# A spectral layer and an MLP on one core: the first forward stage ahead of the weight loads, and later forward stages moved beside their own middle stage

## The chip, the cores and the metric

The kernel runs on one core of one Trainium2 chip. The metric is the device time of one execution in microseconds (us), as the median of several runs of the same program. Everything below is read from one execution that the hardware profiler recorded. PE is the matmul engine (PEld its weight loads), DVE the vector engine, ACT the scalar engine, POOL the GpSimd engine, SP the engine that issues most of the DMAs.

## The reference, cut to what matters

```python
X = np.fft.rfft(x, axis=1)                    # x: 8 batches x 3008 x 256, f32
Yr = Xr @ w_r - Xi @ w_i + b_r                # 256 x 256 complex product per frequency
Yi = Xr @ w_i + Xi @ w_r + b_i
Yr = np.sign(Yr) * np.maximum(np.abs(Yr) - 0.01, 0.0)   # the same for Yi
y = np.fft.irfft(Yr + 1j * Yi, n=3008, axis=1)
h = y.reshape(24064, 256) @ w_in              # 256 x 2048, float64 data
out = np.maximum(0.01 * h, h) @ w_out         # 2048 x 256, float64 data
```

## The kernel before, in words

The transform of 3008 = 47 x 64 points is done as two small transforms. For each batch b there are three pieces of work ahead of the MLP.

- `fwd(b)`, the first stage: x is read as seven column steps c of 2 x 256 columns in two halves h (the last is half as wide). `fold` adds and subtracts the halves, `stage_a` multiplies by the 120 x 120 matrix `fa`, ACT copies the result out of PSUM, and a DMA writes it to the buffer `u_dram` in device memory.
- `mid(b)`, the middle stage: 12 steps j. Each reads a tile `u` back from `u_dram` in another order (`load`), does the second transform (`stage_b`, with `fb`), the complex product with `w_r`, `w_i` (`proj`: `kc`, `t`, `c`, `zf`), the threshold on DVE, the first inverse transform (`stage_g`, with `gb`) and writes `v` to `v_dram`.
- `inverse` and `forms`: read `vin` from `v_dram`, finish the inverse transform, and split 512 tokens into the operands `yh`, `yl` of the MLP.

The MLP (`moe_a`, `moe_b`, `moe_o`) runs over 47 chunks of 512 tokens in eight steps q each. `w_in` and `w_out` arrive as float64 bits and are turned into pairs of f32 by `convert_win` (four quarters, on ACT and DVE) and `load_wout` (eight pieces).

Batches 0 and 1 are prepared ahead (`NPRE` = 2): batch 0 by `f0` and `m0` before the MLP, `fwd(1)` by `fp` in the shadow of `m0`. From then on `Stream` objects hand out the work of later stages in proportion to the progress of the MLP. In the main loop `cur` counts batches; while the MLP passes from one batch to the next, the streams are `fwd(cur + 2)` and then `mid(cur + 1)`. So `fwd(b)` is written one interval ahead of `mid(b)`. The first interval (`cur` = 0) is the shortest: it spans four chunks, its first fifth is left out, and the others span almost six.

Engines run their instructions in the order of the built program, and each DMA queue (SP's and ACT's) issues in order; an instruction that waits holds everything behind it on its engine. The final order is made by a scheduler from the order of the code, so it is shown below from the built programs.

In the part before the MLP the places of interest are: line 648, the first quarter of `w_in` loaded right behind x; lines 664 to 673, the second quarter and the first conversion; lines 676 to 685, the other quarters; line 689, conversions three and four inside `m0`; line 702, `split_consts`, which splits six constants into pairs for the later stages.

Of the kernel before, what the change touches and what calls it, by code (L numbers as in the profile page):

```python
# [8 lines left out]
F32 = mybir.dt.float32  # L9
# [9 lines left out]
N1, N2, NK1 = 47, 64, 24  # L19
# [11 lines left out]
def spectral_mlp_kernel(  # L31
# [173 lines left out]
    XT = [("gf", 2)] + [("gl", 2)] * 2 + [("gh", 2)] * 2 + [("yc", 2)] * 2  # L205
    XT1 = [("yc", 2)] * 2 + [("gf", 2), ("gh", 2), ("yl", 2), ("yh", 2), ("gh", 2)]

    def fwd(b):
# [3 lines left out]
        x_t, s_t = {}, {}  # L212

        def load(c):
            cols = slice(2 * c * D, min(2 * c + 2, NS) * D)
            n = cols.stop - cols.start
            if b < NPRE:
                tag, bufs = (XT, XT1)[b][c]
                x2 = sb.tile([PA, 2, 2 * D], F32, name="xin", tag=tag, bufs=bufs)
                x_t[c] = [x2[:, h, :n] for h in range(2)]  # L220
            else:
                x_t[c] = [
                    sb.tile([PA, 2 * D], F32, name=f"xin{h}", tag="uv"[h], bufs=3 - h)[:, :n] for h in range(2)
                ]
            for h, t in enumerate(x_t[c]):
                if b == 0:
                    (act if h else sync).dma_start(t, x[b, h, :, cols])
                else:
                    with tc.issue_after(reads[-1].ins):
                        sync.dma_start(t, x[b, h, :, cols])  # L230
# [19 lines left out]
        def stage_a(c, h):  # L250
            t = x_t[c][h]
            n = t.shape[1]
            pa = (bank("psf", 2) if b else bank("psh", 4))[:PA, :n]
            products(pa, [(consts[f"fa{h}"] if b else consts[f"fa{h}32"], s_t[c][h])])
            t = x_t[c][1 - h]
            cp = act.copy(t, pa)
            if b == 0:
                turned[:] = [cp]
            st = (act if b else sync).dma_start(uv[h, :, 2 * c * D:2 * c * D + n], t)
            if b == 0:  # L260
                written.append(st)
# [22 lines left out]
        ahead = 2 if b >= NPRE else NX  # L284
        for c in range(ahead):
            load(c)
# [17 lines left out]
    def mid(b):  # L304
# [111 lines left out]
        yield 0  # L416
# [71 lines left out]
    def forms(ci):  # L488
# [7 lines left out]
        def split(k, w):  # L496
            act.copy(yh[:, k], w)  # L497
            return dve.tensor_sub(yl[:, k], w, yh[:, k].bitcast(F32))  # L498
# [12 lines left out]
        if ci == 0:  # L511
            made[:] = [last]
# [135 lines left out]
    load_win(0, (sync, act))  # L648
    load_plain("fb", fb, [P, NK1 + 1, N2])
    load_weights()  # L650
# [6 lines left out]
    sync.dma_start(consts["gb32"][0], gb)  # L657
# [6 lines left out]
    load_win(1, (sync, sync), written[7])  # L664
# [4 lines left out]
    act.copy(bz[:1], brow[:1])  # L669
    act.copy(bz[32:33], brow[32:33])  # L670
    dve.tensor_sub(bz[32:33], brow[32:33], bz[32:33].bitcast(F32))
    act.mul(fa32[:, 2], fa32[:, 1], -1.0)
    convert_win(0)
    m0 = Stream(mid(0), MID)
    m0.to(0.001)
    for c in range(2, 4):
        load_win(c, (sync, sync), reads[3])
# [6 lines left out]
    with tc.issue_after(turned[0].ins):  # L684
        convert_win(1)
# [16 lines left out]
    with tc.issue_after(thresholded[-1].ins):  # L702
        split_consts()
# [3 lines left out]
    next(wout)  # L707


    mids = [Stream(mid(b), MID) for b in range(1, NB)]  # L710
    cur, streams = -1, ()
    for i, pos in enumerate(moe()):
# [3 lines left out]
        if i in (2, 4):  # L716
            with tc.issue_after(made[0].ins):
                next(fp.gen)
        while cur + 1 < NB - 1 and pos >= (read[cur + 1] if cur >= 0 else 0):
# [3 lines left out]
            streams = ([Stream(fwd(cur + NPRE), FWD)] if cur + NPRE < NB else []) + [mids[cur]]  # L723
# [111 lines left out]
```

## Time and profile before

| What | us |
|---|---|
| median of 3 runs | 2609.61 |
| lowest and highest | 2607.25, 2610.03 |
| the profiled execution | 2609.83 |
| its span, first to last instruction | 2608.0 |
| PE busy within the span | 2543.3 |
| DVE, ACT, POOL busy | 1884.8, 1654.5, 248.2 |

The page gives each engine's busy time and share. The table of stretches gives for each stretch the busy time and count of instructions of each engine, the granted clock of the matmul engine as a share of 2.4 GHz, the busy share of the DMA engines and the bytes moved per second. The timeline gives start, duration, engine, line, operation, tiles and count, and in brackets the idle time just before with what ended it. A queue's own issues carry a q (SPq, ACTq).

### The profile page before, as it was taken

To read this page: it belongs to the slowest core of one execution; us is meant where nothing else is said; L and a number is where in the kernel's file an instruction comes from. 1 tells how busy PE (TensorE), PEld (TensorE's weight loads), DVE (VectorE), ACT (ScalarE), POOL (GpSimd) and SP (SyncE) were. 2 spreads that over 40 slices of the span, in tenths; PEclk is the share of its full clock that TensorE was granted. 3 is DMA by queue.
4 is the path that set the end of the run, shared out by engine and by line. 5 is a ranking of instruction groups with operands and counts; after the bars stand their busy time and mean duration, and the time that the engine had idled before them with its cause. 6 is when DMAs were issued, how large, how long until landed. Compare 5 with 4: busy or idle time off the path is not lost.

```text
span 2608.0 us, 42647 instructions
## 1 busy us (share of the span) xinstructions
PE 2543.3 (98%) x16300; PEld 2283.9 (88%) x16300; DVE 1884.8 (72%) x3403; ACT 1654.5 (63%) x3174; POOL 248.2 (10%) x180
## 2 busy tenths in 40 slices
PE   5899999999999999999999999999999999999999
PEld 3678887999989999899999999999999999989998
DVE  6697667777787777777777777777777767667665
ACT  4665665676656666567665766666666666655554
POOL 0002102100120001200021000211000000000000
PEclk8999999999999999999999999999999999999999
DMA  8634113211142112312123111231111111100000
GB/s 248 172 99 116 53 42 92 84 52 47 32 120 61 48 37 56 101 53 59 33 74 94 52 45 41 74 94 52 45 41 53 41 41 44 42 18 32 9 17 17
DMA packets 119914, 165.14 MB, mean 63 GB/s; under 512 B 13602, under 2 KB 69918, under 8 KB 119710
## 3 DMA queue, kind: packets, MB, share of 16 engines
q1 hardware_dynamic: 79120, 115.55, 14.5%
q10 hardware_dynamic: 40589, 46.87, 7.1%
q8 instruction: 128, 2.10, 0.3%
q14 instruction: 77, 0.62, 0.1%
HBM read 86.60 MB, written 75.76 MB: 62 GB/s over the span
## 4 chain that ended last, share of the span: by engine, by line
PE 90%; DVE 3%; ACT 3%; DMA 1%; issue 1%; ACTq 0%; SPq 0%; DVEq 0%
PE pso L568 38%; PE psh L84 34%; PE psf L78 11%; PE psf L472 3%; PE psf L335 3%; DVE gl L555 1%; ACT zf L392 0%; ACT gh L553 0%; ACT gf L551 0%; DMA u_dram<-xin 0%; DVE yl L498 0%; ACT zf L388 0%; DMA raw<-w_out_dram 0%; DVE gf L549 0%; ACTq L412 0%
## 5 line engine op out<-in xcount | busy, mean ns | idle before, releaser
L84 PE MATMUL psh<-yh,win_hi 128*128 128x256 f32 x2632 | 738.4, 285 | 8.1 <-ACT yh L497 4.1
L84 PE MATMUL psh<-yl,win_hi 128*128 128x256 f32 x2632 | 735.1, 281 | 0.0
L84 PE MATMUL psh<-yh,win_lo 128*128 128x256 f32 x2632 | 727.2, 280 | 0.0
L555 DVE TENSOR_TENSOR gl<-gf,gh 128x1024 fp32r<-128x1024 f32 x376 | 475.9, 1266 | 197.5 <-ACT gh L553 195.9
L568 PE MATMUL pso<-gh,wout_hi 128*128 128x512 f32 x1504 | 596.0, 396 | 1.9 <-ACT gh L553 1.8
L568 PE MATMUL pso<-gh,wout_lo 128*128 128x512 f32 x1504 | 591.3, 393 | 0.0
L568 PE MATMUL pso<-gl,wout_hi 128*128 128x512 f32 x1504 | 559.8, 396 | 2.7 <-DVE gl L555 2.4
L84 PEld LDWEIGHTS psh<-yh,win_hi 128*128 128x128 f32 x2632 | 494.3, 189 | 33.6 <-ACT yh L497 5.7
L84 PEld LDWEIGHTS psh<-yl,win_hi 128*128 128x128 f32 x2632 | 497.1, 189 | 25.8 <-issue 0.5
L84 PEld LDWEIGHTS psh<-yh,win_lo 128*128 128x128 f32 x2632 | 493.5, 189 | 4.0 <-issue 0.2
L551 ACT ACTIVATE gf<-gf 128x768 f32<-128x768 f32 x376 | 318.6, 848 | 216.3 <-DVE gf L549 211.3
L553 ACT CAST gh<-gf 128x1024 fp32r<-128x1024 f32 x376 | 395.5, 1052 | 16.5 <-ACT gf L551 10.5
L549 DVE TENSOR_TENSOR gf<-psh,u 128x512 f32<-128x512 f32 x376 | 258.9, 689 | 198.4 <-PE psh L84 196.6
L568 PEld LDWEIGHTS pso<-gl,wout_hi 128*128 128x128 f32 x1504 | 282.5, 188 | 60.7 <-DVE gl L555 7.9
L568 PEld LDWEIGHTS pso<-gh,wout_lo 128*128 128x128 f32 x1504 | 282.9, 188 | 45.1
L568 PEld LDWEIGHTS pso<-gh,wout_hi 128*128 128x128 f32 x1504 | 283.0, 188 | 41.2 <-ACT gh L553 3.0
L548 ACT ACTIVATE gf<-psh 128x256 f32<-128x256 f32 x376 | 144.4, 384 | 214.2 <-PE psh L84 193.0
L371 POOL TENSOR_TENSOR kb<-bias,kc 128x512 f32<-128x512 f32 x84 | 121.4, 1446 | 1468.3 <-ACT kc L368 1302.2
L534 ACT COPY p<-psh 128x256 f32<-128x256 f32 x376 | 139.5, 371 | 100.0 <-PE psh L84 82.2
L535 DVE TENSOR_TENSOR u<-psh,p 128x256 f32<-128x256 f32 x376 | 157.8, 420 | 60.8 <-ACT p L534 58.2
L537 DVE TENSOR_TENSOR gf<-psh,u 128x256 f32<-128x256 f32 x376 | 157.6, 420 | 22.3 <-PE psh L84 11.1
L538 DVE TENSOR_TENSOR gf<-psh,gf 128x256 f32<-128x256 f32 x376 | 158.0, 421 | 6.8
(134 smaller groups left out, 3290.9 us busy)
## 6 DMA issues: line engine op xcount, KB each, us to landing
u<-u_dram SPq DMA_DIRECT2D x192, 128.0 KB, 2.7
v_dram<-v ACTq DMA_DIRECT2D x192, 128.0 KB, 2.4
out_dram<-ob SPq DMA_DIRECT2D x94, 256.0 KB, 2.1
vin<-v_dram SPq DMA_DIRECT2D x96, 240.0 KB, 3.5
xin<-x_dram SPq DMA_DIRECT2D x90, 240.0 KB, 3.0
u_dram<-xin ACTq DMA_DIRECT2D x72, 240.0 KB, 2.4
u_dram<-xin SPq DMA_DIRECT2D x24, 240.0 KB, 4.6
raw<-w_out_dram SPq DMA_DIRECT2D x8, 512.0 KB, 4.9
```

What stands on the lines that cost most here:

```text
L78: last = nc.tensor.matmul(dst, a, b, start=(i == 0), stop=(i == len(terms) - 1))
L84: nc.tensor.matmul(dst, a, b, start=start and i == 0, stop=i == 2, skip_group_check=True)
L534: act.copy(p1, b1[:, lo])
L535: dve.tensor_add(u2, b1[:, hi], p1)
L537: dve.tensor_add(g[:, 3], b2[:, hi], u2)
L538: dve.tensor_add(g[:, 3], b2[:, lo], g[:, 3])
L548: act.activation(g[:, 0], b1[:, lo], AF.Prelu, alpha=SLOPE)
L549: dve.tensor_add(g[:, 1:3], b2.rearrange("p (k n) -> p k n", k=2), u2.unsqueeze(1).broadcast_to([P, 2, HT]))
L551: act.activation(g[:, 1:4], g[:, 1:4], AF.Prelu, alpha=SLOPE)
L553: act.copy(gh, g)
L555: dve.tensor_sub(gl, g, gh.bitcast(F32))
L568: nc.tensor.matmul(po, a[:, f, s], r[:, i], start=(f == 0 and j == 0), stop=(f == NF - 1 and j == 2),)
```

## The change

- `fwd(0)` reads x in four pieces per half (`XW`: 2, 4, 4 and 3 column blocks of 256) in place of seven, one half by ACT's queue and one by SP's; its tiles live in `wide`. The results go back in four writes per half, all on SP's queue. `stage_a` keeps the last copy in `turned` and the last write in `written`.
- No quarter of `w_in` is loaded ahead. All four are loaded from SP's queue: the first behind the read number 3 of `u` (`reads[3]`), the others at `m0` steps 1, 5 and 8. The first conversion comes after the last copy of the first stage, the second and third at steps 5 and 10 of `m0`, the fourth after the last threshold.
- `fb` is loaded in two pieces: five of 25 blocks at the start, the rest behind `reads[3]`. `load_weights` and `gb` come behind the writes of `fwd(0)`. The casts of the bias row and `fa` follow `turned`.
- `split_consts` moves from the end of `m0` into the MLP loop (i = 8), behind the operands of the first chunk.
- For b >= 2 `fwd(b)` becomes part of the same interval as `mid(b)` and stands in front of it: the streams are `fwd(cur + 1)` (none for `cur` = 0) and `mid(cur + 1)`. `mid(b)` hands back 6 x 512 units after its first two loads, a gap for the data to land.

```diff
+    XW = [(0, 2), (2, 6), (6, 10), (10, 13)]
+    XT = ["gf", "gl", "gh", "yc"]
...
+            if b == 0:
+                lo, hi = XW[c]
+                if c == 0:
+                    x2 = sb.tile([PA, 2, 2 * D], F32, name="xin", tag=XT[c])
+                    w = [x2[:, h] for h in range(2)]
+                else:
+                    w = [sb.tile([PA, 4 * D], F32, name="xin", tag=XT[c])[:, :(hi - lo) * D] for _ in range(2)]
+                for h, t in enumerate(w):
+                    (act if h else sync).dma_start(t, x[b, h, :, lo * D:hi * D])
+                for s in range(lo, hi, 2):
+                    x_t[s // 2] = [t[:, (s - lo) * D:min(s + 2 - lo, hi - lo) * D] for t in w]
+                    wide[s // 2] = (w, lo, hi, s + 2 >= hi)
+                return
...
-            st = (act if b else sync).dma_start(uv[h, :, 2 * c * D:2 * c * D + n], t)
-            if b == 0:
-                written.append(st)
+            if b:
+                act.dma_start(uv[h, :, 2 * c * D:2 * c * D + n], t)
+                return
+            turned[:] = [cp]
+            w, lo, hi, last = wide[c]
+            if last:
+                written[:] = [sync.dma_start(uv[h, :, lo * D:hi * D], w[1 - h])]
...
         for j in range(2):
             load(j)
-        yield 0
+        yield 6 * CS if b else 0
...
-    load_win(0, (sync, act))
-    load_plain("fb", fb, [P, NK1 + 1, N2])
-    load_weights()
+    consts["fb"] = const.tile([P, NK1 + 1, N2], F32, name="fb")
+    sync.dma_start(consts["fb"][:, :5], fb[:, :5])
...
-    load_win(1, (sync, sync), written[7])
+    with tc.issue_after(written[0].ins):
+        load_weights()
+        sync.dma_start(consts["gb32"][0], gb)
...
-    convert_win(0)
     m0 = Stream(mid(0), MID)
     m0.to(0.001)
-    for c in range(2, 4):
-        load_win(c, (sync, sync), reads[3])
+    with tc.issue_after(reads[3].ins):
+        sync.dma_start(consts["fb"][:, 5:], fb[:, 5:])
+    load_win(0, (sync, sync), reads[3])
+    with tc.issue_after(turned[0].ins):
+        convert_win(0)
...
-        if i in (3, 8):
-            convert_win(2 + i // 8)
+        if i in (1, 5, 8):
+            load_win(1 + i // 4, (sync, sync), reads[-1])
+        if i in (5, 10):
+            convert_win(i // 5)
...
+    with tc.issue_after(thresholded[-1].ins):
+        convert_win(3)
...
-    with tc.issue_after(thresholded[-1].ins):
-        split_consts()
...
+        if i == 8:
+            with tc.issue_after(made[0].ins), tc.issue_after(made[1].ins):
+                split_consts()
...
-            streams = ([Stream(fwd(cur + NPRE), FWD)] if cur + NPRE < NB else []) + [mids[cur]]
+            streams = ([Stream(fwd(cur + 1), FWD + 4 * CS)] if cur else []) + [mids[cur]]
```

ACT in the first stage, before: the copies of the first stage (`xin<-psh`) with the first conversion's two ACT instructions (`cvq`, `cva`) among them.

```order
L256 COPY xin<-psh 120x512 x5
L123 ACTIVATE cvq<-win_raw 128x1024
L124 ACTIVATE cva<-win_raw 128x1024
L256 COPY xin<-psh 120x512 x5
L104 CAST wr_hi<-w_105 128x512
L669 CAST bz<-brow 1x512
L670 CAST bz<-brow 1x512
L256 COPY xin<-psh 120x512
L104 CAST gb_hi<-w_105 128x128
L256 COPY xin<-psh 120x256 x2
```

ACT at the same place, after.

```order
L268 ACT_TABLE_LOAD
L268 COPY xin<-psh 120x512 x12
L268 COPY xin<-psh 120x256 x2
L684 CAST bz<-brow 1x512
L685 CAST bz<-brow 1x512
L686 ACTIVATE fa_66<-fa_66 120x120
L353 COPY ef<-psh 128x2x256 x2
L123 ACTIVATE cvq<-win_raw 128x1024
L124 ACTIVATE cva<-win_raw 128x1024
L382 COPY kc<-pso 128x256
```

The fourteen copies now stand together; the first conversion stands behind two steps of the middle stage (`ef`) and ahead of the first copy of its product (`kc`).

SP's queue from the writes of the first stage (`u_dram<-xin`) to the first reads of the middle stage (`u<-u_dram`), before.

```order
L259 DMA u_dram<-xin 120x512 x7
L147 DMA win_raw<-w_in_dram 128x1024
L259 DMA u_dram<-xin 120x512 x3
L147 DMA win_raw<-w_in_dram 128x1024
L259 DMA u_dram<-xin 120x512
L259 DMA u_dram<-xin 120x256 x2
L321 DMA u<-u_dram 64x2x256 x6
L147 DMA win_raw<-w_in_dram 128x1024 x4
```

SP's queue there, after.

```order
L275 DMA u_dram<-xin 120x1024 x4
L275 DMA u_dram<-xin 120x768 x2
L113 DMA w_162<-w_r_dram 128x2x256
L113 DMA w_i<-w_i_dram 128x2x256
L678 DMA w_162<-gb_dram 128x128
L335 DMA u<-u_dram 64x2x256 x6
L691 DMA fb<-fb_dram 128x1280
L147 DMA win_raw<-w_in_dram 128x1024 x2
```

The `w_in` loads moved from among the writes to behind the reads; `w_r`, `w_i` and `gb` moved to between the two.

DVE at the end of `mid(0)`, before: the last two thresholds (`t`, `c`), the splits of the constants (`wr_lo` to `fa_lo`) and the last operand of `stage_g` (`zf`).

```order
L380 TENSOR_TENSOR t<-psf,kc 128x512
L383 TENSOR_SCALAR c<-t 128x512
L384 TENSOR_TENSOR t<-t,c 128x512
L105 TENSOR_TENSOR wr_lo<-w_105,wr_hi 128x512
L105 TENSOR_TENSOR wd_lo<-w_105,wd_hi 128x512
L105 TENSOR_TENSOR wn_lo<-w_105,wn_hi 128x512
L105 TENSOR_TENSOR gb_lo<-w_105,gb_hi 128x128
L105 TENSOR_TENSOR fa_lo<-fa_66,fa_hi 120x120 x2
L390 TENSOR_SCALAR zf<-t,sign 64x256 x2
```

DVE there, after.

```order
L394 TENSOR_TENSOR t<-psf,kc 128x512
L397 TENSOR_SCALAR c<-t 128x512
L398 TENSOR_TENSOR t<-t,c 128x512
L125 TENSOR_SCALAR cva<-cva 128x1024
L404 TENSOR_SCALAR zf<-t,sign 64x256 x2
L126 TENSOR_SCALAR cva<-cva 128x1024
L127 SCALAR_TENSOR_TENSOR cva<-win_raw,cva 128x1024
L128 TENSOR_SCALAR win_raw<-cva 128x1024
L125 TENSOR_SCALAR cva<-cva 128x512
```

One instruction of the fourth conversion (`cva`) stands where the six splits stood; the rest of that conversion follows behind `zf`, mixed with the first piece of `w_out`.

## Rows read from the trace of the kernel before

**Rows 1.** The page, part 1: busy time, share of the span, instructions.

```profile
PE 2543.3 (98%) x16300; PEld 2283.9 (88%) x16300; DVE 1884.8 (72%) x3403; ACT 1654.5 (63%) x3174; POOL 248.2 (10%) x180
```

**Rows 2.** Table of stretches by stage; columns in its first line.

```profile
core 0: us, PE busy (x) PEld busy (x) DVE busy (x) ACT busy (x) POOL busy (x), PEclk, DMA share, GB/s
0.00:41.60 41.60, 14.57 (x28) 6.03 (x29) 23.32 (x35) 17.99 (x31) 0.52 (x5) 0.82 0.83 253
41.60:107.80 66.20, 58.04 (x286) 47.30 (x286) 51.59 (x93) 47.76 (x96) 0.30 (x1) 0.94 0.66 186
107.80:134.50 26.70, 25.62 (x85) 13.86 (x86) 13.13 (x28) 14.47 (x32) 0.00 (x0) 0.92 0.69 207
134.50:180.00 45.50, 42.49 (x258) 35.61 (x257) 42.46 (x85) 29.91 (x57) 1.33 (x1) 1.00 0.31 99
...
220.00:480.00 260.00, 240.41 (x1499) 214.10 (x1498) 184.66 (x326) 156.77 (x311) 45.11 (x33) 0.96 0.27 76
```

**Rows 3.** Timeline of ACT in the first stage: start, duration, what.

```profile
18.80 1.12 ACT L123 ACTIVATE cvq<-win_raw 128x1024 f32<-128x1024 uint32 x1 [2.73 <-DMA win_raw<-w_in_dram]
19.82 1.10 ACT L124 ACTIVATE cva<-win_raw 128x1024 f32<-128x1024 f32 x1
20.82 2.53 ACT L256 COPY xin<-psh 120x512 f32<-120x512 f32 x5
```

**Rows 4.** Timeline of SP's queue: the first reads of the middle stage.

```profile
37.88 3.95 SPq L321 DMA_DIRECT2D u<-u_dram  x6
```

**Rows 5.** Table of stretches: DMA rates in the first stage.

```profile
2.00:14.00 12.00, 6.84 (x10) 2.79 (x11) 4.77 (x7) 3.75 (x8) 0.00 (x0) 1.00 0.99 261
14.00:22.00 8.00, 5.42 (x14) 2.13 (x13) 5.30 (x10) 4.73 (x8) 0.00 (x0) 1.00 1.03 349
...
24.00:36.00 12.00, 0.30 (x2) 0.00 (x0) 8.18 (x13) 5.38 (x11) 0.00 (x0) 0.61 0.93 306
```

**Rows 6.** DMA issues of the whole run: count, KB each, median us to landing.

```profile
u<-u_dram SPq DMA_DIRECT2D x192, 128.0 KB, 2.7
...
win_raw<-w_in_dram SPq DMA_DIRECT2D x7, 512.0 KB, 6.5
...
u_dram<-xin ACTq DMA_DIRECT2D x12, 120.0 KB, 2.3
```

**Rows 7.** Table of stretches: inside the middle stage of batch 0, and the sum.

```profile
49.00:84.00 35.00, 32.19 (x167) 25.97 (x166) 30.66 (x54) 26.84 (x55) 0.00 (x0) 1.00 0.85 238
...
sum 66.60, PE 58.04 PEld 47.33 DVE 50.98 ACT 47.51 POOL 0.30; mean PE 19.35 PEld 15.78 DVE 16.99 ACT 15.84 POOL 0.10
```

**Rows 8.** Timeline of DVE at the end of the middle stage.

```profile
103.89 0.69 DVE L384 TENSOR_TENSOR t<-t,c 128x512 f32<-128x512 f32 x1
...
106.99 0.71 DVE L390 TENSOR_SCALAR zf<-t,sign 64x256 f32<-64x256 f32 x2
```

**Rows 9.** Groups of DVE instructions, 38 to 104.6 us: the conversion's first and last.

```profile
L164 DVE TENSOR_TENSOR win_lo<-ws,win_hi 128x1024 fp32r<-128x1024 f32 x3 | 3.7, 1225 | 3.7 <-ACT win_hi L163 3.7
...
L157 DVE TENSOR_TENSOR ws<-cva 128x256 f32<-128x256 f32 x3 | 1.3, 419 | 0.0
```

**Rows 10.** PE's waits, 180 to 480 us: total, times, longest.

```profile
PE psf L78 <- DVE xz L246: 5.1, 4, 2.4
PE psh L84 <- ACT yh L497: 4.1, 2, 3.6
PE psf L78 <- DVE yt L503: 4.0, 1, 4.0
```

**Rows 11.** Chain that ended last: runs of MLP matmuls.

```profile
526.73 3.16 PE psh L84 x27
...
1263.72 2.77 PE pso L568 x12
```

**Rows 12.** Timeline at the end of fwd(2): last copy and its write.

```profile
244.80 0.37 ACT L256 COPY xin<-psf 120x256 f32<-120x256 f32 x1
...
245.21 0.32 ACTq L259 DMA_DIRECT2D u_dram<-xin  x1
```

More of the change, by code (lines that the diff above doesn't have):

```diff
@@ L204, in spectral_mlp_kernel @@
     NX = -(-NS // 2)
-    XT = [("gf", 2)] + [("gl", 2)] * 2 + [("gh", 2)] * 2 + [("yc", 2)] * 2
+    XW = [(0, 2), (2, 6), (6, 10), (10, 13)]
+    XT = ["gf", "gl", "gh", "yc"]
     XT1 = [("yc", 2)] * 2 + [("gf", 2), ("gh", 2), ("yl", 2), ("yh", 2), ("gh", 2)]
@@ L211, in fwd @@
         uv = ud.rearrange("c k (g s) d -> c (k g) (s d)", g=NG)
-        x_t, s_t = {}, {}
+        x_t, s_t, wide = {}, {}, {}
         def load(c):
@@ L216, in load @@
             n = cols.stop - cols.start
+            if b == 0:
[11 more added lines that the diff above has]
+                return
             if b < NPRE:
-                tag, bufs = (XT, XT1)[b][c]
+                tag, bufs = XT1[c]
                 x2 = sb.tile([PA, 2, 2 * D], F32, name="xin", tag=tag, bufs=bufs)
@@ L225, in load @@
             for h, t in enumerate(x_t[c]):
-                if b == 0:
[L227 to L230, printed above, removed]
+                with tc.issue_after(reads[-1].ins) if b == 1 else nullcontext():
+                    sync.dma_start(t, x[b, h, :, cols])
         def fold(c):
@@ L282, in fwd @@
             return
-        ahead = 2 if b >= NPRE else NX
-        for c in range(ahead):
+        ahead = 2 if b else NX
+        for c in range(ahead if b else len(XW)):
             load(c)
@@ L496, in split @@
         def split(k, w):
-            act.copy(yh[:, k], w)
-            return dve.tensor_sub(yl[:, k], w, yh[:, k].bitcast(F32))
+            cp = act.copy(yh[:, k], w)
+            return dve.tensor_sub(yl[:, k], w, yh[:, k].bitcast(F32)), cp
         split(0, b11)
@@ L511, in forms @@
         if ci == 0:
-            made[:] = [last]
+            made[:] = last
         yield
@@ L656, in spectral_mlp_kernel @@
     sync.dma_start(sign, sg)
-    sync.dma_start(consts["gb32"][0], gb)
     bo = sb.tile([P, 2 * D + P], F32R, name="bz", tag="t", bufs=1)
@@ L668, in spectral_mlp_kernel @@
         sb.tile([P, 4, 2, P], F32, name="ws", tag="yh"))
-    act.copy(bz[:1], brow[:1])
-    act.copy(bz[32:33], brow[32:33])
+    with tc.issue_after(turned[0].ins):
+        act.copy(bz[:1], brow[:1])
+        act.copy(bz[32:33], brow[32:33])
+        act.mul(fa32[:, 2], fa32[:, 1], -1.0)
     dve.tensor_sub(bz[32:33], brow[32:33], bz[32:33].bitcast(F32))
-    act.mul(fa32[:, 2], fa32[:, 1], -1.0)
-    convert_win(0)
     m0 = Stream(mid(0), MID)
     m0.to(0.001)
-    for c in range(2, 4):
-        load_win(c, (sync, sync), reads[3])
+    with tc.issue_after(reads[3].ins):
+        sync.dma_start(consts["fb"][:, 5:], fb[:, 5:])
+    load_win(0, (sync, sync), reads[3])
+    with tc.issue_after(turned[0].ins):
+        convert_win(0)
     bias = const.tile([P, 2, D], F32, name="bias")
@@ L683, in spectral_mlp_kernel @@
     fp = Stream(fwd(1), FWD)
-    with tc.issue_after(turned[0].ins):
-        convert_win(1)
     wout = load_wout()
@@ L706, in spectral_mlp_kernel @@
     next(wout)
-    next(wout)
-    mids = [Stream(mid(b), MID) for b in range(1, NB)]
+    mids = [Stream(mid(b), MID + 6 * CS) for b in range(1, NB)]
     cur, streams = -1, ()
```

3 lines of the change are left out of this document (removed).

## The prediction

> **What bounds the kernel now.** I read the page's busy table first. PE is busy 2543.3 us of 2608.0 [rows 1], so the end is set by PE's work, which the change leaves as it is (the built programs hold the same matmuls), and by the 64.7 us in which PE is idle, plus what it loses at half clock. So I look for where the idle time lies; the table of stretches answers [rows 2]. Up to 41.6 us PE works 14.6 us and idles 27.0. In the middle stage of batch 0 (41.6 to 107.8) it idles 8.2. While the MLP begins it idles 1.1 and 3.0, in 220 to 480 us 19.6, and 5.8 remain for all the rest. A reader should see two targets there, the start and the stretch 220 to 480, and nothing to win after 480.
>
> The start has a chain. ACT stands still 2.73 us for the first quarter of `w_in` and then converts for 2.2 us, with copies of the first stage queued behind [rows 3]. The DMA engines are busy 93 to 103% in the stretches of [rows 5], since `w_in` and `fb` share them with x and its results. Only when the last result is written does SP issue the first reads of the middle stage, at 37.88 us [rows 4].
>
> The waits of PE in 180 to 480 us [rows 10] are on DVE's and ACT's work for `fwd(2)`, `fwd(3)`, `mid(1)` and the next chunk: the first interval is the densest. The mean granted clock is 0.96 in 220 to 480 [rows 2]; two-level clock gives 260 x 0.04 x 2 = 21 us at 1.2 GHz, after such waits of 3.6 and 4.0 us. Some of it is idle anyway; I put the loss at 6 us, 26 in all with the idle time.
>
> **The change part by part.** The sum is made against the profiled 2609.83 us (span 2608.0 and 1.8 around it), 0.2 above the median of the runs.
>
> *First reads of the middle stage.* `w_in`, most of `fb` and `w_r`, `w_i` no longer stand before them. x is 13 blocks x 2 halves x 120 rows x 1 KB = 3.19 MB in, the same out, with `fa` and a fifth of `fb` 6.67 MB in all. The transfers begin near 2 us, and from the end of the last full stretch (36) to the read passed 1.9 us. At 261 GB/s (narrow x rows alone), 306 (mostly narrow writes) and 349 (with the wide rows of `w_in`) [rows 5] the bytes take 25.6, 21.8 or 19.1 us, and the read comes at 29.5, 25.7 or 23.0. I take 25.7, because half the bytes are writes as in the 306 stretch: **-12.2** (-8.4 to -14.9). The engines are not later than this: fourteen copies at 2.53/5 = 0.5 us [rows 3] follow x, which is in by 2 + 3.47/0.306 = 13.3 us, so the last write can be issued near 18, and its 0.74 MB end before 22.
>
> Rates in the trace are those of many queued transfers: 306 GB/s with pieces of 240 KB, all engines at 0.93 [rows 5]. The Trainium skill (DMA: Bandwidth & Descriptors, Bandwidth) gives for single transfers 138 GB/s at 64 KB and 341 at 1 MB and asks for 1 MiB and more. By that rule the pieces of 480 KB win more: at 341 GB/s the read would come at 2 + 19.6 + 1.9 = 23.5, an estimate from that page, and the time be 2.2 us lower. The trace does not bear it out, since its 240 KB pieces are well above what the page's table would give them.
>
> *Length of the middle stage.* Before, 66.7 us from the first read (37.88) to the end of the last threshold (104.58) [rows 4, 8]. Now the first conversion has to wait for its data behind the reads. SP issues six reads in 3.95 us [rows 4], `fb` and the two `w_in` loads at the same 0.66 each, and a `w_in` load lands 6.5 us after issue [rows 6]: some 11.8 us after the first read. Then the two ACT instructions, 2.2 us [rows 3]; DVE starts to convert at 14.0. While ACT waits, the copy `kc` of step 0 is queued behind it, on that DVE's threshold and the PSUM banks of PE's next products; but that `kc` is ready only near then, after two steps. DVE still has three conversions and twelve steps to do, as before: 51.0 us of work, the sum in [rows 7]. At the 30.66/35.00 = 88% of the busiest stretch [rows 7] that is 58.2 us, an end at 72.2: **+5.5**. If PE's pace hides it, 0 (the steps need 58 us of PE [rows 7]); at the mean share 50.98/66.60 the end is at 80.6, +13.9. I take 88%, as the conversions now fill the stage to its end.
>
> *Splits.* The six splits stand between 104.58 and 106.99 on DVE, ahead of the last `zf` [rows 8]. One instruction of the fourth conversion takes their place; a conversion's cost 0.4 to 1.2 us each [rows 9]. **-1.7** (-1.2 to -2.0). The start: -12.2 + 5.5 - 1.7 = **-8.4**.
>
> *Where the MLP begins.* The fourth conversion (twelve groups, 29.3 us for three, 9.8 each; the first and last are [rows 9]) now runs after the last threshold. DVE has 26.7 - 13.1 = 13.6 idle us there [rows 2], and PE meanwhile has `fwd(1)` to multiply, so most is covered. The splits (2.4 us) and one of the pieces of `w_out` slip into 134.5 to 180, where DVE is busy 42.46 of 45.50 and PE already waits 3.0 [rows 2]. **+2**, the splits' size (0 to +7: with a piece of `w_out`, seven DVE instructions of half the width, at 0.4 to 0.7 each [rows 9] 3 to 5 us).
>
> *First interval.* `fwd(2)` leaves it; `mid(1)` is handed out over more MLP. In the built orders, from its first `stage_b` to its last, PE has 132 us of matmuls before and 169 after, counted at 3.16/27 = 0.117 us for 256 columns and 2.77/12 = 0.231 for 512 [rows 11]; `fwd(2)` itself goes from 51 to 60. In later intervals of before a middle stage has about 190 and almost nothing is lost. So much of the 26 us should go. But the order still has tight places: at two steps only 2.4 us of matmuls between `stage_b` and the product that needs it, where before the tightest were 0.0 and 1.0; and once no matmul between the last `inverse` and the next chunk. **-10** (0 to -20, which is 26 less three waits of 2).
>
> *Six handovers.* `mid(b)` now reads what `fwd(b)` has just written. The read waits on SP's queue, ahead of output stores, `vin` and x loads. The chain: the last matmul 0.12 [rows 11], 0.41 from its copy to the issue of the write [rows 12], landing 2.3 [rows 6], a second half of the read 0.66 behind the first [rows 4], landing 2.7 [rows 6]: 6.2. The order gives 4.5, 8.1, 6.3, 6.9, 7.9 and 6.8 us of matmuls between (the first is 12 x 0.231 + 15 x 0.117), so one handover of six is short, by 1.7. **+3** with some half clock (0 to +20, if each read took the 6.5 of a `w_in` load).
>
> Sum: -8.4 + 2 - 10 + 3 = -13.4, from 2609.8 to 2596.4, or 2596 on the median.
>
> **The rivals.** *Slower: the handovers stall.* If each of the six costs 3 us of waiting and 2 of half clock, as the waits of 3.6 and 4.0 us did [rows 10], that is +30 in place of +3: 2623. For it: nothing in the kernel before reads so soon after a write except the first stage, where the read passed 1.9 us after the bytes thinned out and PE sat idle. Against: later the DMA engines are lightly used (share 0.27 in 220 to 480 [rows 2]). It decides above (8.4 - 2 + 10)/6 = 2.7 us each. Chance 0.12.
>
> *The conversions give the start back.* The same `w_in` bytes and conversions only move into the middle stage, where the DMA share is 0.85 and DVE at 88% in 49 to 84 us [rows 7]. Late reads of `u` would hold ACT and DVE in order: +13.9 for -12.2, and with the MLP's begin at +5 and only -6 in the first interval: -12.2 + 13.9 - 1.7 + 5 - 6 + 3 = +2, 2612. Against: DMA traffic is thin in the last third of the stage. Chance 0.17.
>
> *All of it works.* The read at 23.0, no longer middle stage, all but three waits gone, no handover short: -14.9 - 1.7 - 20 = -36.6, 2573; I count all below 2586 to it. Chance 0.16.
>
> **How the numbers follow.** The forecast, 2586 to 2604, has 0.55 (a slow DMA, with the read at 29.5, still gives 2600). With the rivals' 0.12, 0.17 and 0.16 that is all. A measurement of this kernel tells some 0.2%, 5.2 us, from no change: 2604.4 to 2614.8 is "same". Faster: 0.55 + 0.16 + 0.03 of the second rival = 0.74; same 0.14, the rest of the second; slower 0.12. The range leaves out the lower part of the good case and the slow rival: 2580 to 2612.
>
> **What would show it.** The first reads of `u` on SP's timeline near 25.7 us; no conversion among ACT's copies. The last threshold near 25.7 + 72 = 98, the first long run of MLP matmuls some 8 us earlier than 134.5. PE's idle time in 220 to 480 us near 10, and in each later interval a wait of `stage_b` on `u` of at most 2 us. The prediction is wrong if the reads come after 30 us, if the middle stage exceeds 80 us, or if `stage_b` waits more than 2.7 us at every handover.

## The result and the profile after

The changed kernel takes 2619.59 us (median of 6 runs, 2613.38 to 2620.83), the kernel before 2609.42 beside it: a ratio of 1.0036 [1.0024, 1.0048], slower by some 10 us where 13 us less had been forecast. The profiled execution is the shortest of the six, 2613.38 us with a span of 2611.6; what stands below accounts for its 3.6 us, and of the five longer runs no trace was kept.

Part 1 of the page, as [rows 1], and the same stretches as [rows 2]:

```profile
PE 2555.1 (98%) x16300; PEld 2284.0 (87%) x16300; DVE 1855.0 (71%) x3403; ACT 1655.3 (63%) x3174; POOL 236.7 (9%) x180
```

```profile
107.80:134.50 26.70, 24.70 (x81) 12.75 (x79) 9.97 (x23) 15.04 (x33) 0.00 (x0) 0.94 0.70 208
134.50:180.00 45.50, 39.30 (x225) 34.61 (x226) 40.76 (x86) 29.35 (x56) 0.00 (x0) 0.89 0.19 57
...
220.00:480.00 260.00, 255.95 (x1665) 232.24 (x1664) 190.64 (x343) 168.54 (x330) 36.00 (x27) 0.99 0.24 69
480.00:2500.00 2020.00, 2013.89 (x13183) 1828.76 (x13182) 1452.94 (x2673) 1301.49 (x2508) 198.59 (x146) 1.00 0.19 55
```

The matmuls are the same 16300 and PE is idle for 56.5 us instead of 64.7, yet the span is longer: PE is "busy" 11.8 us more. So the idle column cannot say where the time went. What can is a comparison at equal work. The traces hold the start of every matmul; I gave each kind of matmul one duration (the 30% quantile of its start-to-start distances over all traces compared) and added these in each kernel's own order. The table shows how many us a kernel is ahead of the kernel before when it has done the same matmul work. The columns are the times at which the kernel before is there: the last threshold is past, the MLP has run 70 us, the first intervals are over, the streams begin their last interval, only MLP is left, the last matmul. They are worked out from one profiled execution each, and these scatter: after, start_only, after_pin and c_lastint have the same order of matmuls up to 111 us, and at 109 us they stand 2.8 to 7.1 ahead.

| ahead at | 109 | 198 | 534 | 2056 | 2341 | 2604 |
|---|---|---|---|---|---|---|
| after | 7.1 | -7.4 | 16.9 | 16.5 | 13.1 | -3.7 |
| start_only | 2.8 | -13.9 | -17.5 | -17.2 | -17.2 | -17.2 |
| later_only | -0.6 | 1.3 | 27.8 | 27.6 | 24.3 | 7.3 |
| after_pin | 4.9 | -7.7 | 16.8 | 16.4 | 13.5 | 13.9 |
| c_lastint | 4.2 | -9.9 | 13.0 | 12.3 | 12.9 | 13.2 |
| later_pin | 0.3 | 0.4 | 27.0 | 26.5 | 23.7 | 24.0 |
| later_lastint | 1.4 | 2.0 | 28.3 | 26.8 | 27.4 | 27.7 |
| c_split_pin | -0.9 | -4.3 | 21.0 | 20.2 | 17.4 | 17.7 |
| turn4_pin | 8.9 | 0.9 | 25.3 | 24.5 | 21.7 | 22.1 |
| mended | 4.9 | -0.9 | 24.5 | 23.9 | 24.4 | 24.8 |

The changed kernel is 7 us ahead after the start, loses 14.5 where the MLP begins (12.6 to 16.7 in the four), wins 24.3 in the first intervals and keeps it for 1500 us. Then it gives away 3.4 in the last interval and 16.8 in the last 270 us, where only MLP is left and the two programs hold the same code.

There the stretch 2400 to 2500 us shows it best (before first, then after):

```profile
2400.00:2500.00 100.00, 100.00 (x645) 90.60 (x644) 68.42 (x124) 56.31 (x100) 0.00 (x0) 1.00 0.05 17
```

```profile
2400.00:2500.00 100.00, 98.95 (x622) 87.38 (x621) 60.13 (x112) 51.79 (x96) 0.00 (x0) 1.00 0.03 11
```

Clock 1.00 in both, PE busy 100.00 and 98.95, but 622 matmuls in place of 645: 3.6% less work at 1% less busy time. The weight loads (PEld) show it, 87.38 us in place of 90.60, also 3.6%. The Trainium skill (Perfetto Trace Analysis, Identifying the Most-Contended Engine) warns of this: matmuls are pipelined, so their busy share is no good measure, and that of the weight loads is a better one. The trace agrees. The timelines of PE, ACT and DVE of the changed kernel at one such place:

```profile
2453.95 0.28 PE L84 MATMUL psh<-yh,win_lo 128*128 128x256 f32 x1
2454.38 0.50 PE L582 MATMUL pso<-gh,wout_hi 128*128 128x512 f32 x1 [0.15 <-ACT gh L567]
2454.72 0.39 PE L582 MATMUL pso<-gh,wout_lo 128*128 128x512 f32 x1
...
2455.18 0.40 PE L582 MATMUL pso<-gh,wout_lo 128*128 128x512 f32 x1
2455.64 0.50 PE L582 MATMUL pso<-gl,wout_hi 128*128 128x512 f32 x1
```

```profile
2453.30 1.03 ACT L567 CAST gh<-gf 128x1024 fp32r<-128x1024 f32 x1
```

```profile
2454.36 1.23 DVE L569 TENSOR_TENSOR gl<-gf,gh 128x1024 fp32r<-128x1024 f32 x1 [1.54 <-ACT gh L567]
```

The starts tell it, not the gaps: elsewhere in these rows a 256-column matmul is followed by the next after 0.12 us, a 512-column one after 0.23. Here the first output matmul starts 0.43 us behind the one before it, when ACT has cast `gh` (2453.30 + 1.03), the next 0.34 behind that, the first that needs `gl` 0.46 behind its neighbour, since DVE makes `gl` only after `gh`, and the one behind it 0.34. Of these 0.76 us in excess the view calls 0.15 idle. The reason is the order on PE. One step of the MLP is a (12 matmuls), b (9), then H (8 from `gh`) and L (4 from `gl`). In the tail, counted in matmuls:

```
before: b357x6 a358x4 H356x4 a359x5 L356 H356 .. b358x3 a359x7 b358x6 H357x4 L357 H357 ..
after:  b356x6 b357x6 a358x6 a359x12 b358x3 H356x4 L356 H356 .. H357x4 b359x3 a360x6 L357 ..
```

Before, H of a step comes when the next step's b is done, one step at a time. After, the b of two steps stand together and then the H and L of both: a **pair**. H356 follows its own b after 27 matmuls, 3.2 us, and between the two lie an activation, an addition, another activation and the cast. In chunks 38 to 46 the order of the changed kernel holds 34 pairs, that of before 12; in the last five chunks it is 19 and 1.

### The profile page after: what moved, and what is told of

It is laid out like the page before. It is cut to its first block, busy times and chain, and to the rows that moved or that the text cites. A ratio compares the mean times of both kernels' runs of the same rounds, so it can differ in the third digit from the quotient of the medians.

```text
span 2611.6 us, 42622 instructions
## 1 busy us (share of the span) xinstructions
PE 2555.1 (98%) x16300; PEld 2284.0 (87%) x16300; DVE 1855.0 (71%) x3403; ACT 1655.3 (63%) x3174; POOL 236.7 (9%) x180
## 5 line engine op out<-in xcount | busy, mean ns | idle before, releaser
L569 DVE TENSOR_TENSOR gl<-gf,gh 128x1024 fp32r<-128x1024 f32 x376 | 466.0, 1240 | 194.0 <-ACT gh L567 192.2
L84 PEld LDWEIGHTS psh<-yl,win_hi 128*128 128x128 f32 x2632 | 497.6, 189 | 23.7 <-DVE yl L512 1.9
L582 PEld LDWEIGHTS pso<-gl,wout_hi 128*128 128x128 f32 x1504 | 282.7, 188 | 67.7 <-DVE gl L569 12.6
L551 DVE TENSOR_TENSOR gf<-psh,u 128x256 f32<-128x256 f32 x376 | 155.8, 418 | 21.0 <-PE psh L84 11.8
```

The costliest lines, as they stand in the source:

```text
L84: nc.tensor.matmul(dst, a, b, start=start and i == 0, stop=i == 2, skip_group_check=True)
L551: dve.tensor_add(g[:, 3], b2[:, hi], u2)
L569: dve.tensor_sub(gl, g, gh.bitcast(F32))
L582: nc.tensor.matmul(po, a[:, f, s], r[:, i], start=(f == 0 and j == 0), stop=(f == NF - 1 and j == 2),)
```

## Experiments

Each time is a median with the ratio to the kernel before that ran beside it. That kernel took 2606.5 us beside start_split, mended, wide_lastint and later_lastint_pinall and 2608.9 to 2610.5 beside the others, so a difference of some us between rows is better read from the ratios (0.001 is 2.6 us).

| kernel | us | ratio |
|---|---|---|
| start_only | 2623.31 | 1.0057 [1.0044, 1.0069] |
| later_only | 2602.54 | 0.9974 [0.9965, 0.9984] |
| after_pin | 2599.60 | 0.9962 [0.9949, 0.9974] |
| c_lastint | 2596.54 | 0.9947 [0.9934, 0.9959] |
| c_split_pin | 2591.88 | 0.9937 [0.9923, 0.9951] |
| turn4_pin | 2589.84 | 0.9927 [0.9914, 0.9939] |
| later_pin | 2585.31 | 0.9913 [0.9899, 0.9926] |
| later_lastint | 2582.38 | 0.9900 [0.9887, 0.9914] |
| start_split | 2620.61 | 1.0051 [1.0038, 1.0063] |
| mended | 2588.48 | 0.9928 [0.9914, 0.9941] |
| wide_lastint | 2585.35 | 0.9916 [0.9903, 0.9930] |
| later_lastint_pinall | 2589.01 | 0.9929 [0.9916, 0.9943] |
| mended_early | 2589.32 | 0.9925 [0.9912, 0.9937] |
| mended_no4 | 2586.51 | 0.9907 [0.9892, 0.9923] |
| later_no4 | 2580.40 | 0.9893 [0.9879, 0.9906] |
| mended_w2 | 2586.84 | 0.9915 [0.9901, 0.9928] |
| mended_early_w2 | 2588.90 | 0.9920 [0.9907, 0.9934] |
| later_w3 | 2586.57 | 0.9910 [0.9897, 0.9924] |

**The two halves.** The change falls apart into its start and its later part.

```diff
 start_only = after with
-            streams = ([Stream(fwd(cur + 1), FWD + 4 * CS)] if cur else []) + [mids[cur]]
+            streams = ([Stream(fwd(cur + NPRE), FWD)] if cur + NPRE < NB else []) + [mids[cur]]
 and MID, yield 0 as before; later_only = before with the opposite
```

> The change's start alone; the streams, their totals and the wait before the middle stages are put back as before. At equal matmul work done the changed kernel is 1 us ahead at 107 us, 10 us behind at 225 us, 14 us ahead from 500 to 2070 us, and 4 us behind at the end. Theory A (the end is lost by the order of the tail's matmuls, which here is that of before): no loss after 2070 us; the loss of 11 us between 107 and 225 us belongs to this part and shows here, so between 2604 us (given back by the stalls of the first interval) and 2619 us (2609.5 + 10). Rival B (the whole loss is the start's): 2617 us or more. Rival C (the start's gain of 5 us is kept to the end): 2602 to 2605 us.

> The change's later part alone: first stages beside their own middle stage, the start as before. Its order has the same tail as the changed kernel, in which two steps' hidden products stand together and then both steps' output products (four pairs a chunk from chunk 39 on, against none to three before). Theory A (tail's order): the first interval gains about 20 us, the tail loses about 13 us after 2250 us and 3 us in the last interval, as in the changed kernel: 2600 to 2607 us, with 2 to 2.5 us a chunk lost over the last 8 chunks against the kernel before. Rival B (the loss is the start's): no loss in the tail, about 2590 us.

The start alone costs 14 us, more than theory A had allowed (2619 at most): in its profiled execution, the slowest of the five, 17 us are lost by 534 us and nothing after. The later part alone gains 7, though it is 28 us ahead for most of the run: its order has the same tail as the changed kernel, and it falls from 24.3 to 7.3 there. So the tail's loss comes with the later part: start_only's time is the one of rival B, but B has no loss in the tail of later_only. C falls too.

**The order of the tail.** Held by an order on PE alone:

```diff
+                with tc.issue_after(hidden[0].ins) if ci >= 38 else nullcontext():
+                    moe_o(*steps[i - LAG], 0)
```

where `hidden[0]` is the last matmul of the latest b. In the second kernel nothing of the tail is touched; `fwd(7)` goes back to the interval before the last, behind `mid(6)`:

```diff
+            if cur == NB - 3:
+                ahead.append(NB - 1)
```

> The changed kernel; from chunk 38 on the output products of a step are issued behind the hidden products of the next one, as an order among TensorE's own instructions, no wait on another engine. The order then holds 1 pair in the last 9 chunks in place of 34. Theory A (the order of the tail costs it): 2606 to 2608 us less, if only the pairs go, than the 2619.6 us of the changed kernel by 12 to 13 us, so 2605 to 2608 us in median, with the last chunk back from 55 to about 48 us. Rival D (the tail is slow for another reason, such as ScalarE and VectorE being late whatever the order): within 2 us of the changed kernel, 2617 to 2622 us.

(The first half of that sentence on theory A miscounts; 2605 to 2608 was meant.)

> The changed kernel, with the last first stage alone back in the interval before, behind the middle stage there, so that the last interval holds one middle stage, as before the change. Nothing in the tail is touched, but the scheduler's order of it holds 1 pair in the last 9 chunks in place of 34. Theory A (order of the tail): 2603 to 2608 us, the tail's loss of 13 us gone and that of 3.6 us in the last interval perhaps too. Rival D (the tail is slow whatever the order): 2616 to 2622 us.

2599.6 and 2596.5: 20 and 23 us less than the changed kernel (17.4 and 16.7 in the profiled executions), and by the medians more than was expected of either. Rival D falls twice, by two edits that share only the order they lead to. At 2400 to 2500 us after_pin, then c_lastint:

```profile
2400.00:2500.00 100.00, 100.00 (x640) 90.40 (x639) 64.82 (x115) 55.39 (x98) 0.00 (x0) 1.00 0.04 13
```

```profile
2400.00:2500.00 100.00, 100.00 (x637) 90.34 (x636) 64.78 (x116) 55.92 (x98) 0.00 (x0) 1.00 0.04 15
```

PE's waits in the tail, 2330 to 2588 us, of later_only; in after_pin, c_lastint and later_pin this list is empty there:

```profile
PE pso L568 <- ACT gh L553: 2.8, 15, 0.5
```

The same two edits on the later part alone:

> The later part of the change alone (2602.5 us) with the tail's order held as in after_pin. Theory A (order of the tail): at equal work later_only is 27 us ahead of the kernel before from 450 to 2050 us, loses 3.4 us in the last interval and 12.4 us behind 2250 us and the rest at the last matmuls; with the order held only the 3.4 us go, so 2609.2 less 22 to 24 us: 2585 to 2588 us. Rival D (the tail is slow for another reason, or the gain of after_pin was the start's): 2598 to 2603 us.

> The later part alone (2602.5 us) with the last first stage put back in the interval before. Its order holds 1 pair in the last 9 chunks without being held. Theory A: the tail's 16 us and the last interval's 3.4 us are both kept, less what the interval before loses by two first stages (0 to 4 us): 2582 to 2588 us. Rival D: 2596 to 2603 us.

2585.3 and 2582.4, as theory A said. In the table they keep 24.0 and 27.7 us to the end; the 3 us of the last interval are lost in later_pin and not in later_lastint, where `fwd(7)` has left it. **later_lastint is the fastest complete kernel here** by its median, 1.0% under the kernel before; the interval of its ratio overlaps those of later_pin and wide_lastint.

Holding the order in every chunk (`if True` in place of `ci >= 38`) was meant to carry this further.

> later_lastint (2582.4 us) with the order of after_pin held in every chunk, not from chunk 38 on. Steps whose output products come within 3.7 us of their last hidden product go from 34 to 11. At 0.6 us a step (0.3 us of wait for gh, 0.3 us for gl in the tail's rows) that is up to 14 us: 2568 to 2580 us if such steps wait in the middle of the run as they do in the tail; 2580 to 2585 us if there the transforms between them already fill the time.

It is 6.6 us slower than later_lastint, outside both ranges. At equal work its profiled execution, the slowest of five, stands within 3 us of that one to 1750 us and is 11 us behind at 2040; it loses them in the interval with two first stages, where PE's waits of 1840 to 2060 us begin with

```profile
PE psh L84 <- ACT yh L498: 2.1, 3, 1.2
PE psf L78 <- DVE xz L248: 1.2, 1, 1.2
```

while later_lastint has 0.2 us there. So in the middle of the run the held order gained nothing and lost time in that interval; that pairs cost time is shown for the tail alone.

**What the start loses.** The splits now stand behind the first chunk's operands. The raw weights lie in one of the two buffers of `yl` until they are split, so the first `yl` of the MLP takes the other, which holds the fifth tile of `fwd(1)`, one of the last to be transformed. DVE of the changed kernel, groups of 118 to 140 us, the first `yl` and one group of the splits; then the first `yl` of before on its timeline:

```profile
L512 DVE TENSOR_TENSOR yl<-yc,yh 128x512 fp32r<-128x512 f32 (+1 forms) x3 | 1.7, 601 | 7.1 <-ACT xin L286 6.4 <-ACT yh L511 0.7
L105 DVE TENSOR_TENSOR wr_lo<-w,wr_hi 128x512 fp32r<-128x512 f32 x1 | 0.7, 686 | 0.0
```

```profile
128.25 0.41 DVE L498 TENSOR_TENSOR yl<-yc,yh 128x256 fp32r<-128x256 f32 x1
```

What comes of it on PE stands in its timeline: a wait for DVE's `u`, the sum of the first step of the MLP, and behind it matmuls of 256 columns that start 0.21 us apart in place of 0.12.

```profile
142.18 0.39 PE L84 MATMUL psh<-yh,win_hi 128*128 128x256 f32 x1 [2.77 <-DVE u L549]
...
144.08 0.41 PE L84 MATMUL psh<-yh,win_hi 128*128 128x256 f32 x1
144.29 0.41 PE L84 MATMUL psh<-yl,win_hi 128*128 128x256 f32 x1
144.50 0.41 PE L84 MATMUL psh<-yh,win_lo 128*128 128x256 f32 x1
```

One kernel puts `split_consts()` back behind the last threshold; the other leaves it late and transforms that tile third:

```diff
-            for c in (0, 1, 2, 3, 6, 4, 5):
+            for c in (0, 1, 4, 2, 3, 6, 5):
```

> The changed kernel with the tail's order held as in after_pin (2599.6 us), and the splitting of the first spectrum's constants put back behind the last threshold, ahead of the MLP's first operands. The raw weights stand in one of the two buffers of yl until they are split, so with the late split the MLP's first yl takes the buffer of the second batch's fifth transform tile and VectorE waits for it: 6.4 us in the changed kernel, to 134.2 us, and 3.6 us of splits follow at 137 to 141 us. Theory E (that is what the start loses, 11 us behind later_only between 128 and 206 us of equal work): 2590 to 2595 us, the first yl near 129 us. Rival F (the four late quarters of w_in, converted between 101 and 116 us, are what costs): within 3 us of 2599.6 us, or slower by the 1.7 to 3.6 us of splits.

> after_pin (2599.6 us) with the second batch's fifth tile, the one that holds the buffer of yl, transformed third and not sixth; the splits stay late. Theory E: the 4.9 to 6.4 us wait of the first yl goes, the splits' 3.6 us on VectorE stay: 2594 to 2598 us. Rival F (the late quarters of w_in): no change, 2598 to 2601 us.

7.7 and 9.8 us less than after_pin by the medians, 3.8 and 8.2 in the profiled executions: the buffer is what costs, since turn4_pin leaves the splits where they are. The stretch 134.5 to 150 us of before, after, after_pin, c_split_pin and turn4_pin shows it; the granted clock, which has the two levels 1.2 and 2.4 GHz, is down in the two that wait for the buffer:

```profile
134.50:150.00 15.50, 13.56 (x89) 10.86 (x87) 12.88 (x29) 9.46 (x21) 0.00 (x0) 1.00 0.55 171
134.50:150.00 15.50, 11.13 (x65) 10.14 (x66) 14.81 (x37) 10.17 (x25) 0.00 (x0) 0.78 0.22 65
134.50:150.00 15.50, 11.24 (x65) 9.74 (x63) 14.47 (x35) 10.23 (x26) 0.00 (x0) 0.78 0.23 65
134.50:150.00 15.50, 14.25 (x89) 10.99 (x88) 13.07 (x31) 9.23 (x22) 0.00 (x0) 1.00 0.50 144
134.50:150.00 15.50, 13.35 (x81) 11.38 (x80) 15.50 (x35) 11.11 (x24) 0.00 (x0) 1.00 0.17 49
```

At equal work the changed kernel loses 8.0 us between 140 and 146 us (times of the kernel before), c_split_pin nothing and turn4_pin 2.2. The first `yl` of turn4_pin on DVE's timeline, against 134.16 in the changed kernel:

```profile
120.33 0.42 DVE L513 TENSOR_TENSOR yl<-yc,yh 128x256 fp32r<-128x256 f32 x1 [3.99 <-ACT yh L512]
```

It beats its expectation by 4 us. But both fall short of later_pin, which has nothing of the new start. With the old streams:

> start_only (2623.3 us, 14 us slower than the kernel before) with the splits of the first spectrum's constants put back behind the last threshold. Theory E (late splits hold a buffer of yl and then stand on VectorE ahead of the first steps; worth 7.7 us on top of after_pin): 2612 to 2617 us; what is left against 2609 us is then the four quarters of w_in, the last converted at 101 to 113 us and w_out's eight conversions pushed from 115-188 to 115-205 us. Rival F (w_in's late quarters carry all of it): 2620 to 2624 us. Rival G (the start part without its late splits gains what it was made for, 5 us at the last threshold): 2604 to 2608 us.

2620.6 against 2623.3, within the intervals of each other; the expectation of theory E fails here, and the time lies in rival F's range. The profiled executions, a slow one of start_only and a short one of start_split, are 7.2 us apart; in the latter start_split is 10 us behind the kernel before, some 5 of it by 198 us.

**What is left.** All mends together (splits back, tile third, `fwd(7)` back), and the wide rows alone on top of later_lastint:

> The whole changed kernel with three lines put back or moved: splits behind the last threshold, the second batch's fifth tile third, the last first stage one interval earlier. Theories A and E with what they left over (2.5 to 6 us of later w_out conversions against later_pin): 2583 to 2588 us, no faster than later_lastint (2582.4 us), so the moved start would gain nothing. Rival G (the earlier end of the first middle stage comes through once the buffer wait is gone): 2576 to 2580 us.

> later_lastint (2582.4 us) with the wide rows of the first stage alone: reads of 2 to 4 row pairs, u written in four pieces by SyncE, while w_in, fb and the weights stay where they were before the change. Rival G (an earlier first stage ends the start earlier and the MLP with it): 2576 to 2580 us. Theory E (the start is bound by the conversions of w_in and w_out that stand behind one another on VectorE and ScalarE until the MLP, not by the first stage): 2580 to 2585 us, whatever the middle stage's first read gains.

2588.5 and 2585.4, 6 and 3 us over later_lastint, 7 and 4 by the ratios: the times of rival G were not reached. But neither kernel tests it, since in neither does the first middle stage end earlier. Its last threshold ends at 104.8 us in mended and 108.2 in wide_lastint, against 99.25 in the changed kernel and 103.2 in later_lastint. With the splits put back, a cast of theirs comes to the head of ACT's order, and three of its four loads of x stand behind it (mended, then the changed kernel):

```profile
3.53 0.29 ACT L104 CAST fa_hi<-fa 120x120 fp32r<-120x120 f32 x1 [0.43 <-DMA fa<-fa_dram]
3.54 1.94 ACTq L227 DMA_DIRECT2D xin<-x_dram  x3
```

```profile
1.82 3.76 ACTq L227 DMA_DIRECT2D xin<-x_dram  x3
```

The last copy of the first stage ends at 27.0 us in mended and at 21.7 in the changed kernel. In all seven kernels with the new start and the splits back the three loads start at 3.4 to 3.8 us, the last copy ends at 25.6 to 27.5 and the last threshold at 104.8 to 108.8; in the five with late splits these are 1.8, 21.7 to 24.0 and 99.3 to 103.6. So the splits put back free the buffer and lose the earlier start; that these casts are the reason is argued from the order, no run moves them alone.

mended is 4.9 us ahead at 109 us and 0.9 behind at 198. The conversions were the next suspect; `mended_early` reads and converts all four quarters of `w_in` inside the middle stage (`load_win` for c in 0 to 3 behind `reads[3]`, `convert_win` at i = 3, 6, 9), two kernels leave the arithmetic of the last quarter out, and three move steps of `w_out` (the change had also taken one of two `next(wout)` ahead of the MLP):

> mended (2588.5 us) with all four quarters of w_in read as soon as the first four reads of u are issued and converted inside the first middle stage, as before the change (there 29.7 to 87.5 us; in the changed kernel 52.9 to 112.7 us). Theory H (what the start still costs after the splits, 6 us against later_lastint, is the conversions that end after the last threshold and push w_out's into the MLP): 2578 to 2584 us, w_out's last conversion back near 190 us. Rival J (it costs something else, or the reads of w_in now slow the reads of u and the gain goes into a longer middle stage): 2586 to 2590 us.

> mended (2588.5 us) without the arithmetic of w_in's last quarter: its operands are filled with a constant by GpSimd at the start, the reads stay. Theory H: the 9 us of VectorE and 4 us of ScalarE between 101 and 113 us go, w_out's conversions come earlier: 2579 to 2584 us. Rival J: 2586 to 2589 us.

> later_lastint (2582.4 us) without the arithmetic of w_in's last quarter, as a control for mended_no4. There the conversion lies inside the first middle stage and ends at 88 us. Theory H: it is covered there, 2580 to 2583 us. If the middle stage itself waits for VectorE, up to 5 us less, 2577 us.

> mended (2588.5 us) with the second conversion of w_out put back ahead of the MLP: the change also took one of the two steps of w_out that stood there. In mended the last of the eight conversions ends at 194 us and in later_lastint at 185 us; at equal work mended falls 3.3 us behind between 160 and 180 us and 2.5 us more between 385 and 400 us. Theory K (that step, on VectorE and ScalarE among the first steps of the MLP, is what is left): 2582 to 2585 us, the last conversion near 186 us. Rival J (something else): 2586 to 2590 us.

> mended_early (2589.3 us) with the same step of w_out put back: the changed start with wide rows, and every conversion where it stood before. Theory K: 2581 to 2585 us. Rival G (the start then gains its 5 us): 2577 to 2580 us. Rival J: 2586 to 2590 us.

> later_lastint (2582.4 us) with a third step of w_out ahead of the MLP. Theory K turned round (each step taken out of the MLP's first stretch gives 3 to 5 us as long as it is covered ahead of it): 2577 to 2582 us. If VectorE and ScalarE are full there, or the third raw piece isn't there yet: 2582 to 2588 us.

mended_early: no gain, against theory H. Leaving the quarter out: 2.0 us in mended and 2.0 in the control by the medians, but 0.0021 and 0.0007 (5.5 and 1.8 us) by the ratios, each with some 0.0015 either way; at equal work mended_no4 ends no better than mended. Theory H is not borne out, and these two do not exclude a part of it. The step of `w_out` put back: the last instruction of its conversions starts at 190.2 us in place of 193.9, and the time is 1.6 us less, by the ratios 0.0013 with intervals of that size; mended_early_w2 stays at 2588.9, and one more step ahead makes later_lastint slower, not faster (4 us by the medians, 0.0010 by ratios whose intervals overlap). Theory K's times are not reached. The table at other moments shows why: between 170 and 198 us mended loses 3.1 us and mended_w2 nothing, but before that, between 130 and 160 us, mended loses 2.6 and mended_w2 7.4. What the step saves there it costs earlier. What the mended start still costs against later_lastint, 3 us by 198 us and 4 by 534 in the profiled executions and 6 in the medians, **stays open** beyond this, and so does what the changed start would be worth with its early reads kept and the buffer free.

## Why the prediction was wrong

Two steps of the sum failed: the beginning of the MLP, where a buffer was held, and the stretches after 480 us, where the order of untouched code changed. In the order of the sum, with what the table measured for the profiled execution:

- *First reads.* At 27.16 us, against 37.88 [rows 4] and 25.7 predicted: -10.7 in place of -12.2. SP's queue of the changed kernel:

```profile
16.58 7.07 SPq L275 DMA_DIRECT2D u_dram<-xin  x7
23.70 1.23 SPq L113 DMA_DIRECT2D w<-w_r_dram  x1
24.98 1.48 SPq L113 DMA_DIRECT2D w_i<-w_i_dram  x1
26.50 0.50 SPq L678 DMA_DIRECT2D w<-gb_dram  x1
27.16 1.31 SPq L335 DMA_DIRECT2D u<-u_dram  x2
```

  I had the last write issued near 18 and left the three loads ahead of the reads out, some 3 us on the queue. The writes' issues ended at 23.65 (16.58 + 7.07), since the copies of the first stage came 0.86 us apart and not 0.5, each behind PE:

```profile
18.70 0.58 ACT L268 COPY xin<-psh 120x512 f32<-120x512 f32 x1 [0.27 <-PE psh L78]
19.56 0.58 ACT L268 COPY xin<-psh 120x512 f32<-120x512 f32 x1 [0.27 <-PE psh L78]
```

  So it was the engines and the queue that set the read, where the sum had the bytes at 306 GB/s and the engines "not later than this"; that it came out within 1.5 us is luck. The larger pieces didn't move faster: 262, 235 and 321 GB/s in 2 to 14, 14 to 21 and 21 to 27 us, where [rows 5] have 261, 349 and 306. The estimate of 23.5 us by the Trainium skill (DMA: Bandwidth & Descriptors, Bandwidth) is not borne out by this trace.
- *Length of the middle stage.* The last threshold ends at 98.56 + 0.69 = 99.25, so 72.1 us; predicted 72.2 (73.3 to 75.3 in the other four kernels with late splits). The working holds too: DVE begins to convert 13.7 us after the first read (14.0 predicted) and is then busy 85% of the time to the end (88%). The end on DVE's timeline, and that stretch:

```profile
98.56 0.69 DVE L398 TENSOR_TENSOR t<-t,c 128x512 f32<-128x512 f32 x1
99.17 0.69 DVE L125 TENSOR_SCALAR cva<-cva 128x1024 f32<-128x1024 f32 x1
99.89 0.72 DVE L404 TENSOR_SCALAR zf<-t,sign 64x256 f32<-64x256 f32 x2
```

```profile
41.20:99.25 58.05, 49.89 (x246) 38.85 (x244) 49.21 (x86) 47.17 (x93) 0.30 (x1) 1.00 0.73 205
```

- *Splits.* -1.7 predicted, -1.8 measured: PE's last product of the stage, which needs the last `zf`, starts 3.27 us behind the end of the last threshold before and 1.50 after. PE's wait for it is 2.6 us in place of 4.4 (before, then after):

```profile
107.85 2.05 PE L78 MATMUL psh<-zf,w 128*128 128x512 f32 x2 [4.39 <-DVE zf L390]
```

```profile
100.75 2.04 PE L78 MATMUL psh<-zf,w 128*128 128x512 f32 x2 [2.63 <-ACT zf L402]
```

  The start as a whole: -10.7 + 5.4 - 1.8 = -7.1, as in the table, 8.4 predicted. This part held, within the scatter of 2.8 to 7.1.
- *Where the MLP begins.* **Failed.** Predicted +2 (0 to +7), measured 7.1 + 7.4 = 14.5. I counted the instructions that move into it and DVE's idle time, but not what the moved splits hold: a buffer of `yl`. DVE stood idle for 6.4 us in order, waiting for the fifth tile; then PE waited 2.77 us and ran on at a granted clock of 0.78, and for the clock the sum had nothing there. That is 8.0 us between 140 and 146, and the two kernels that free the buffer lose 0 and 2.2 there. Another 5.4 us go between 170 and 198. The piece of `w_out` that the range allowed at 3 to 5 us fits them, and mended_w2 shows 3 us for it, but no run takes it out of the changed kernel alone.
- *First interval.* -10 predicted, -24.3 measured, beyond the -20 of the range: PE 255.95 of 260 busy at clock 0.99, against 240.41 and 0.96 [rows 2]. Right in kind: nearly all of the 26 us went, where the sum let 16 of them stay for tight places in the order.
- *Handovers.* +3 predicted, 0.4 measured (16.9 to 16.5 over 1500 us). Of the six only the first, which falls into the first interval's column, shows in PE's list (230 to 600 us) a wait for a read of `u`, 0.5 us where 1.7 was predicted:

```profile
PE psf L349 <- DMA u<-u_dram: 0.5, 1, 0.5
```

  The slower rival, at 2.7 us each, fell; the time came out on its side by another way.
- *Nothing to win after 480 us.* **Failed**, and this turns the sign: 3.4 us in the last interval and 16.8 in the tail, both not in the sum. I read idle time, in which nothing was to be won there, and took stretches whose code the diff leaves alone as fixed. But the built order is made anew from the whole program, and the order shows the pairs before anything runs. I had compared it at the handovers only.

The terms, all differences of one row of the table, add up to -7.1 + 14.5 - 24.3 + 0.4 + 3.4 + 16.8 = +3.7, against 2613.38 - 2609.83 = 3.55. Without the tail's pairs the changed kernel is after_pin, 2599.6 us, inside the range; but that is luck in part, since 12.5 us too little at the beginning of the MLP and 14.3 us too little gained in the first interval nearly cancel. The 6 us between the profiled execution and the median of the changed kernel are not explained.

## What to carry to other kernels

A change to a scheduled program moves work where no line was touched: compare the built order of the whole run, not only around the edit, and count instructions per stretch rather than busy time. Of an instruction that is moved later, ask which buffer its operands hold until then, and who takes that buffer next. Two kernels that are to be compared are best laid against each other at equal work done; that separates a gain that is kept from one that is given back later. And of a mend that disappoints, ask whether the gain that it should free is still there: here it had moved other work ahead of the first loads.

## What the runs showed beyond that

- A wait of 0.76 us in a row of matmuls showed as 0.15 us of idle time, and a stretch with 3.6% fewer matmuls as 98.95% busy.
- The order of the last 72 of 376 steps decided 17 us by the traces and 20 by the medians.
- A late buffer cost twice: 2.77 us of waiting on PE, and behind it matmuls 0.21 us apart in place of 0.12.
- The same mend (splits back) was worth 7.7 us with the new streams and 2.7 with the old ones by the medians, but 3.8 and 7.2 in the profiled executions: these runs don't tell whether such gains add.
